# Batch 0's first two x pieces by another queue and another engine, filter copies between bt copies, and w1 - w2 in quarters

## The chip, the cores and the metric

The kernel runs on one core of a Trainium2 chip. The metric is the device time of one execution in microseconds; a profiled execution also gives a span, from the first to the last instruction that its trace holds. The engines are called TensorE (PE in the profile; its weight loads are PEld), VectorE (DVE), ScalarE (ACT), GpSimd (POOL) and SyncE (SP). DMAs are issued by SyncE (queue q1 in the profile) and by GpSimd (queue q0); both share the core's 16 DMA engines.

## What is computed

Eight batches of 3072 tokens with 256 channels are filtered along the sequence in the frequency domain, and the result goes through a max-out layer:

```python
X = np.fft.rfft(x, axis=1)
Y = X * (filt_r + 1j * filt_i)
y = np.fft.irfft(Y, n=3072, axis=1)          # 8 x 3072 x 256
g = np.maximum(y @ w1, y @ w2)               # 256 -> 1024
out = g @ w_out                              # 1024 -> 256
```

Since max(a, b) = b + max(a - b, 0), the kernel needs one wide product: y @ (w1 - w2), a Relu, the product with w_out, and y @ M with M = w2 @ w_out.

## The kernel before

**Tiling.** A sequence of 3072 is split as 96 x 32. The transform is two matmul stages with tables (`C1`, `U`), a product with the filter `F`, and two stages back (`VP` and `VQ`, then `G1`). Batch 1 is transformed while batch 0 goes through the max-out layer, batch 2 while batch 1 does, and so on. The tables, batch 0's whole transform and the weights come first, and nothing runs beside them: this is the prologue, the code from line 143 to line 651. After it the loop at line 693 runs 64 steps of 384 tokens, each with eight `moe_h` (L448, the product with `Wd` = w1 - w2) and the thirty matmuls of `moe_o` (L474 and L476) for the step before. The order of the program is written by hand, and each engine executes its own instructions in that order.

**The prologue in its order.**

- GpSimd issues eight DMAs of batch 0's x (`load_x`, L88), each 96 rows of 1024 numbers, cast from float32 to bfloat16 on the way, with the index tables (iota) between them. Then come 18 DMAs of the filter (`load_f`, L117, L120, L124): ten for the part `WP[0]` (frequency blocks w = 0 to 7), eight for `WP[1]` (w = 8 to 11). Then the first quarter of batch 1's x (L172).
- VectorE builds the angles of `C1` (L176 to L184) and of `U` (L201 to L239). The latter need four small ScalarE results `t2` (L219).
- ScalarE computes `C1` by a sine (L185), those four, and later the two halves of `U` (L243).
- `s1t(c)` for c = 0 to 7 (L495): eight matmuls of an x piece with `C1`, and two evictions (L505 on ScalarE, L503 on VectorE for the last two pieces) into `at2`. `spin` puts filler matmuls between them.
- `t1(n)` for n = 0 to 5 (L507) transposes `at2`; VectorE (even n, L516) and ScalarE (odd n, L514) copy the results to `bt`.
- The filter has to stand on 64 partitions although 32 are loaded: `double_f` copies the other 32, by four VectorE copies for `WP[0]` (L130) and by four SyncE DMAs for `WP[1]` (L132). `fix_f` (L140) sets one row.
- `s2` (L376) makes `px`; the products with `F` (L382, L388, L389) are shared between VectorE, which reads `px` in PSUM, and GpSimd, which reads a copy `xs` that ScalarE makes (L593). GpSimd has v = 0, 2, 3, 4 and half of 5.
- `s3t`, `t2` and `s4` lead to the first tile of y, which the first `moe_h` reads.
- GpSimd, after its last product, issues two quarters of batch 1's x (L633), makes the first half of `Wd` (`prep_wd(0, G)`, L292, 128 x 1024 numbers), issues `Wo` (L288) and the last quarter of batch 1's x, makes the second half of `Wd`, and then the table `CT`.

**What reads these.** `moe_h(0, j)` reads 128 columns of `Wd`: j = 0 to 3 the first half, 4 to 7 the second. The first `moe_o` and `prep_m` (L306) read `Wo`. `f1(1, c)` (L324) reads batch 1's x: c = 0 to 3 the first quarter, 4 to 7 the second, and so on; c = 4 comes in step 3 of the loop, c = 8 in step 6.

```python
    def prep_wd(h, engine):
        js = slice(512 * h, 512 * h + 512)
        engine.tensor_tensor(Wd[:, :, js], w1f[:, :, js], w2f[:, :, js], OP.subtract)
```

Of the kernel before, what the change touches and what calls it, by code (L numbers as in the profile page):

```python
# [10 lines left out]
AF = mybir.ActivationFunctionType  # L11
# [6 lines left out]
NP = 96  # L18
NM = 32
# [7 lines left out]
def kernel(  # L27
# [14 lines left out]
    nc = tc.nc  # L42
    V, S, G, TE = nc.vector, nc.scalar, nc.gpsimd, nc.tensor
# [20 lines left out]
    XF = [const.tile([128, 2, 2, D], FP32, name="XF%d" % k) for k in range(3)]  # L64
# [11 lines left out]
    xb = {}  # L76

    def x_tile(b, c):
        if c % 2 == 0:
            xb[b] = xpool.tile([128, 8, D], BF16, tag="xb", name="xb")  # L80
        return xb[b][:, 4 * (c % 2):4 * (c % 2) + 4]

    def load_x(b, c, n):
        for k in range(c, c + n):
            xb[b, k] = x_tile(b, k)[0:NP]
        src = x[b].rearrange("(p m) d -> p m d", m=NM)
        m0 = 4 * (c % 2)
        G.dma_start(out=xb[b][0:NP, m0:m0 + 4 * n], in_=src[:, 4 * c:4 * c + 4 * n, :])  # L88

    def load_xf(b, c):  # L90
        src = x[b].rearrange("(h p m) d -> p h m d", h=2, m=NM)
        for g in range(2):
            nc.sync.dma_start(out=XF[(8 * b + c) % 3][64 * g:64 * g + 48],
                              in_=src[:, :, 4 * c + 2 * g:4 * c + 2 * g + 2, :])
            if b == 2 and c < 3:

                nc.sync.dma_start(out=XF[(8 * b + c) % 3][64 * g + 48:64 * g + 64],
                                  in_=src[0:16, :, 4 * c + 2 * g:4 * c + 2 * g + 2, :])
# [27 lines left out]
    def double_f(h, g, ri, engine):  # L126
        w0, w1 = WP[h]
        o_, i_ = F[64 * g + 32:64 * g + 64, ri, w0:w1], F[64 * g:64 * g + 32, ri, w0:w1]
        if engine is V:
            V.tensor_copy(o_, i_)  # L130
        else:
            nc.sync.dma_start(out=o_, in_=i_)  # L132
# [3 lines left out]
    def load_fn():  # L136
        nc.sync.dma_start(out=FN[32:33], in_=filt_r[1536:1537, :])

    def fix_f():
        V.tensor_copy(F[32:33, 0, 0, 0], FN[32:33])  # L140
# [9 lines left out]
    cid = init.tile([128, 128], FP32)  # L150

    hv = init.tile([128, 2, 1], FP32)
    load_x(0, 0, 1)
    G.iota(pid, pattern=[[1, 1]], base=0, channel_multiplier=1, allow_small_or_imprecise_dtypes=True)
    G.iota(kc, pattern=[[2, NW], [24, 2], [1, 2]], base=0, channel_multiplier=0,
           allow_small_or_imprecise_dtypes=True)
    load_x(0, 1, 1)
    G.iota(kap, pattern=[[2, NW], [24, 2]], base=0, channel_multiplier=0,
           allow_small_or_imprecise_dtypes=True)
    G.iota(jb, pattern=[[1, 16]], base=0, channel_multiplier=0, allow_small_or_imprecise_dtypes=True)  # L160
    load_x(0, 2, 1)
    G.iota(cid, pattern=[[1, 128]], base=0, channel_multiplier=0, allow_small_or_imprecise_dtypes=True)
    for c in range(3, 8):
        load_x(0, c, 1)
    for q in range(2):
        G.memset(hv[:, q], 1.0)
# [2 lines left out]
    load_f(0)  # L169
    load_f(1)  # L170
    load_fn()
    load_x(1, 0, 2)  # L172

    def table_c():
        p96 = init.tile([128, 1], FP32)
        V.tensor_scalar(p96, pid, 1.0 / 96.0, None, OP.mult)  # L176
        uc = init.tile([NP, 48, 2], FP32)
        rc = init.tile([NP, 48, 2], FP32)
        kf = kc.rearrange("p w g s -> p (w g s)")
        V.tensor_scalar(uc[:, :, 0], kf, p96[0:NP], 0.25, OP.mult, OP.add)  # L180
        V.tensor_scalar(uc[:, :, 1], kf, p96[0:NP], None, OP.mult)
        V.tensor_scalar(uc[:, 0:1, 1], pid[0:NP], 0.5, 0.25, OP.mult, OP.add)
        V.tensor_scalar(rc, uc, RND, RND, OP.add, OP.subtract)
        V.tensor_tensor(uc, uc, rc, OP.subtract)  # L184
        S.activation(C1, uc.rearrange("p k r -> p (k r)"), AF.Sin, bias=zero[0:NP], scale=TWO_PI)  # L185

    def table_ct():
        G.memset(CT, 0.0)
        for g in range(2):
            G.tensor_copy(CT[64 * g:64 * g + 48, :, 0:48].rearrange("p s (u r) -> p s u r", r=2),  # L190
                          C1[0:48].rearrange("p (u s r) -> p s u r", s=2, r=2))
# [49 lines left out]
    def sines_u(h):  # L241
        uv = ua.rearrange("p u c s j -> p u (c s j)")
        S.activation(U[:, NW * h:NW * h + NW], uv[:, NW * h:NW * h + NW], AF.Sin, bias=zero, scale=TWO_PI)  # L243

    def table_g():
        pg = ps.tile([96, NP], FP32, tag="ps", name="pg")
        TE.matmul(pg, C1, I128[0:NP, 0:NP], start=True, stop=True)
        S.activation(G1, pg, AF.Copy)
# [30 lines left out]
    def load_w(h):  # L279
        js = slice(512 * h, 512 * h + 512)  # L280
        nc.sync.dma_start(out=w1f[:, :, js], in_=moe_w1.rearrange("(c p) j -> p c j", p=128)[:, :, js])
        nc.sync.dma_start(out=w2f[:, :, js], in_=moe_w2.rearrange("(c p) j -> p c j", p=128)[:, :, js])
# [4 lines left out]
    def load_wo():  # L287
        G.dma_start(out=Wo, in_=moe_w_out.rearrange("(c p) j -> p c j", p=128))  # L288

    def prep_wd(h, engine):  # L290
        js = slice(512 * h, 512 * h + 512)
        engine.tensor_tensor(Wd[:, :, js], w1f[:, :, js], w2f[:, :, js], OP.subtract)  # L292

    def prep_t(jp):
# [212 lines left out]
    def t1(n, engine):  # L507
        pb = ps.tile([128, 4, D], BF16, tag="ps", name="pb")
        for i in range(4):
            for dc in range(2):  # L510
                TE.transpose(pb[:, i, 128 * dc:128 * dc + 128],
                             at2[:, dc, 4 * n + i].rearrange("p q m -> p (q m)"), I128)
        if engine is S:
            S.activation(bt[0][:, 4 * n:4 * n + 4], pb, AF.Copy)  # L514
        else:
            V.tensor_copy(bt[0][:, 4 * n:4 * n + 4], pb)  # L516

    def s3t(v, pq):
        pool, tag = (ps, "ps") if v % 2 else (pso, "po")
        pz = [pool.tile([128, 2, 2, 2, 2, NM], FP32, tag=tag, name="pt%d" % g) for g in range(2)]  # L520
        for _ in range(2 if v == 1 else 1):
            TE.matmul(pz[0].rearrange("p i s r c m -> p (i s r c m)"), W1[:, 0:128], W1, start=True, stop=True)
        for i in range(2):
            for s in range(2):
                for dc in range(2):
                    for q, tab in enumerate((VP, VQ)):
                        for g in range(2):
                            TE.matmul(pz[g][:, i, s, :, dc], pq[s][64 * g:64 * g + 64, q, i, 128 * dc:128 * dc + 128],  # L528
                                      tab[64 * g:64 * g + 64, 2 * v + i, s].rearrange("p (r m) -> p r m", r=2),
                                      start=(q == 0), stop=(q == 1))  # L530
        zv = zT.rearrange("p c m (w g) q -> p w g (c m) q", g=2)
        for g in range(2):
            o_ = zv[:, 2 * v:2 * v + 2, g]
            i_ = pz[g].rearrange("p i s r c m -> p i (c m) (s r)")
            if v >= 4 and g == 1:
                V.tensor_copy(o_, i_)
            else:
                S.activation(o_, i_, AF.Copy)
# [17 lines left out]
    def spin(n):  # L556
        for _ in range(n):
            pd = ps.tile([128, 512], FP32, tag="ps", name="pd")
            TE.matmul(pd, W1[:, 0:128], W1, start=True, stop=True)  # L559
# [8 lines left out]
            double_f(1, g, ri, nc.sync)  # L568
    for h in range(2):
        load_w(h)  # L570
    spin(12)
    for c in range(8):
        s1t(c)
        if c == 0:
            table_g()
        if c == 4:
            sines_u(0)
        if c < 7:
            spin(2)
    bt[0] = bpool.tile([128, NU, D], BF16, tag="bt", name="bt")  # L580
    for n in range(6):
        t1(n, S if n % 2 else V)
    put_v(0, 0, table_v(0, 0))
    for g in range(2):
        for ri in range(2):
            double_f(0, g, ri, V)
            if g == 0 and ri == 0:
                fix_f()
    xs = {}

    def stage_x(v):
# [6 lines left out]
    def products(v):  # L598
        pool = pq0 if v > 2 else pqpool
        pq = [product(V, v, 0, pxs[v][0], pool)]  # L600
        if v == 5:
            pq.append(shared_product(v, 1, pxs[v][1], xs[v], pool))
        else:
            pq.append(product(G, v, 1, xs[v], pool) if v in POOLED else product(V, v, 1, pxs[v][1], pool))
        return pq
# [11 lines left out]
    put_v(1, 1, table_v(1, 1))  # L617
    for v in (1, 0, 2):
        pqs[v] = products(v)
    s3t(1, pqs[1])  # L620
    pxs[4] = s2(0, 4)
    stage_x(4)
# [7 lines left out]
        pqs[v] = products(v)  # L630
    for v in (4, 5):
        s3t(v, pqs[v])
    for c in (2, 4):  # L633
        load_x(1, c, 2)
    prep_wd(0, G)
    load_wo()
    load_x(1, 6, 2)
    prep_wd(1, G)
    table_ct()
    setup.close()  # L640
    apool = ctx.enter_context(tc.tile_pool(name="apool", bufs=3))
# [51 lines left out]
    for tt in range(8 * B + 1):  # L693
        b, i = divmod(tt, 8)
        k = 0
        for j in range(8):
# [5 lines left out]
            if tt > 0:  # L702
                n = 3 if j in (3, 7) else 4
# [36 lines left out]
```

## Time and profile before

| | us |
|---|---|
| median of 3 runs | 504.27 (502.98 to 505.7) |
| the profiled execution | 503.8 |
| its span | 502.0 |
| TensorE busy in the span | 488.4 (97%) |
| TensorE busy, first 50 us | 40.25 |
| TensorE busy, 50 to 60 us | 10.00 of 10 |
| VectorE, ScalarE, GpSimd busy in the span | 331.9, 308.3, 257.5 |

A line of the timeline gives start, duration, engine, source line, operation, what it writes and reads, and in brackets the idle time of that engine before it and what ended it. The chain of waits is followed back from the last instruction; each piece has a start, a duration and what ran or was waited for.

### The profile page before, as it was taken

To read this page: it belongs to the slowest core of one execution; us is meant where nothing else is said; L and a number is where in the kernel's file an instruction comes from. 1 tells how busy PE (TensorE), PEld (TensorE's weight loads), DVE (VectorE), ACT (ScalarE), POOL (GpSimd) and SP (SyncE) were. 2 spreads that over 40 slices of the span, in tenths; PEclk is the share of its full clock that TensorE was granted. 3 is DMA by queue.
4 is the path that set the end of the run, shared out by engine and by line. 5 is a ranking of instruction groups with operands and counts; after the bars stand their busy time and mean duration, and the time that the engine had idled before them with its cause. 6 is when DMAs were issued, how large, how long until landed. Compare 5 with 4: busy or idle time off the path is not lost.

```text
span 502.0 us, 13079 instructions
## 1 busy us (share of the span) xinstructions
PE 488.4 (97%) x5299; PEld 362.1 (72%) x5303; DVE 331.9 (66%) x518; ACT 308.3 (61%) x629; POOL 257.5 (51%) x338
## 2 busy tenths in 40 slices
PE   8688999999999999999999999999999999999997
PEld 3455777777777777777777777777777777777775
DVE  7876688457865777457765687557765687555553
ACT  6776478647774676557764586647774465544442
POOL 7893569547463864645654855537632221222220
PEclk9989999999999999999999999999999999999999
DMA  7999789995799667986779558896769235411112
GB/s 125 150 252 217 230 229 290 306 274 171 212 268 260 175 204 234 250 229 189 198 244 275 187 177 245 235 239 197 197 181 255 78 111 153 168 65 64 64 64 84
DMA packets 77966, 97.20 MB, mean 194 GB/s; under 512 B 8017, under 2 KB 54354, under 8 KB 77842
## 3 DMA queue, kind: packets, MB, share of 16 engines
q1 hardware_dynamic: 64642, 66.73, 49.6%
q0 software_dynamic: 13264, 29.64, 20.3%
q8 instruction: 41, 0.67, 0.6%
q14 instruction: 19, 0.16, 0.1%
HBM read 53.87 MB, written 47.19 MB: 201 GB/s over the span
## 4 chain that ended last, share of the span: by engine, by line
PE 90%; DMA 5%; POOL 2%; issue 1%; ACT 1%; DVE 0%; SPq 0%; POOLq 0%; DVEq 0%
PE po L476 34%; PE ph L448 33%; PE po L474 8%; PE pz L399 5%; PE py L428 4%; PE pa L349 2%; DMA F<-in_filt_r_dram 2%; PE px L376 2%; DMA Wo<-in_moe_w_out_dram 2%; POOL xb L88 1%; DMA F<-F 1%; PE pr L549 1%; POOL pq L382 0%; PE pt L528 0%; PE pm__1132 L306 0%
## 5 line engine op out<-in xcount | busy, mean ns | idle before, releaser
L476 PE MATMUL po<-Wo,gt 128*128 128x256 bf16 x1536 | 261.0, 273 | 0.2 <-DMA Wo<-in_moe_w_out_dram 0.2
L452 ACT ACTIVATE gt<-ph 128x384 bf16<-128x384 f32 x321 | 157.0, 496 | 147.9 <-PE ph L448 147.3
L461 POOL DMA_DIRECT2D out_dram<-ot x186 | 102.6, 555 | 187.1 <-DVE ot L488 184.4
L476 PEld LDWEIGHTS <-gt 128*128 128x128 bf16 x1536 | 146.6, 98 | 66.1 <-issue 10.3
L450 DVE TENSOR_SCALAR gt<-ph 128x384 bf16<-128x384 f32 x191 | 104.9, 552 | 63.1 <-PE ph L448 59.9
L382 DVE TENSOR_TENSOR pq<-px,F 128x1024 bf16<-128x1024 f32 x91 | 107.0, 1219 | 24.2 <-PE px L376 22.6
L448 PEld LDWEIGHTS <-Wd 128*128 128x128 bf16 x1024 | 96.5, 98 | 12.9 <-POOL Wd L292 1.4
L103 POOL TENSOR_TENSOR xb<-XF 128x512 bf16<-128x512 f32 x48 | 61.2, 1276 | 41.3 <-DMA XF<-in_x_dram 21.2
L488 DVE COPY ot<-po 128x512 f32<-128x512 f32 x95 | 65.1, 685 | 25.3 <-PE po L476 25.0
L104 POOL TENSOR_TENSOR xb<-XF 128x512 bf16<-128x512 f32 x48 | 61.0, 1271 | 0.0
L403 ACT ACTIVATE zt<-pz 128x512 bf16<-128x512 f32 x84 | 45.6, 595 | 11.5 <-PE pz L399 8.4
L353 ACT ACTIVATE at<-pa 128x512 bf16<-128x512 f32 x96 | 51.8, 610 | 1.2 <-PE pa L349 0.8
L428 PE MATMUL py<-G,zr 96*128 96x96 bf16 x512 | 32.7, 206 | 0.2
L428 PEld LDWEIGHTS <-zr 96*128 96x128 bf16 x512 | 29.0, 97 | 2.5 <-DVE zr L552 0.4
L399 PE MATMUL pz<-pq,VP 64*64 64x256 bf16 x336 | 21.9, 281 | 0.0
L376 PE MATMUL px<-bt,U 64*64 64x256 bf16 x384 | 19.8, 278 | 1.2 <-ACT VQ L273 0.7
L399 PE MATMUL pz<-pq,VQ 64*64 64x256 bf16 x336 | 20.9, 269 | 0.0
L349 PE MATMUL pa<-xb,CT 64*64 64x512 bf16 x192 | 19.5, 383 | 0.0
L399 PEld LDWEIGHTS <-VP 64*64 64x64 bf16 x336 | 9.7, 105 | 13.3 <-issue 13.3
L376 PEld LDWEIGHTS <-U 64*64 64x64 bf16 x384 | 10.4, 109 | 3.9 <-issue 3.3
L559 PE MATMUL pd<-W 128*128 128x512 bf16 x30 | 10.5, 462 | 1.7 <-DVE zero L145 1.5
L552 DVE COPY zr<-pr 96x1024 bf16<-96x1024 bf16 (+1 forms) x8 | 5.2, 649 | 8.0 <-PE pr L549 8.0
(429 smaller groups left out, 609.7 us busy)
## 6 DMA issues: line engine op xcount, KB each, us to landing
out_dram<-ot POOLq DMA_DIRECT2D x186, 128.0 KB, 3.3
XF<-in_x_dram SPq DMA_DIRECT2D x96, 192.0 KB, 4.6
ad<-at SPq DMA_DIRECT2D x56, 192.0 KB, 3.3
bt<-ad SPq DMA_DIRECT2D x14, 768.0 KB, 9.1
zd<-zt SPq DMA_DIRECT2D x42, 256.0 KB, 2.7
zr<-zd SPq DMA_DIRECT2D x56, 192.0 KB, 4.8
WS<-in_moe_w_dram SPq DMA_DIRECT2D x4, 512.0 KB, 5.1
xb<-in_x_dram POOLq DMA_DIRECT2D x8, 192.0 KB, 5.8
```

Of the source, the lines that this page charges most:

```text
L103: G.tensor_tensor(t_[:, 0], f[:, 0], f[:, 1], OP.add)
L104: G.tensor_tensor(t_[:, 1], f[:, 0], f[:, 1], OP.subtract)
L353: S.activation(at[:, m0:m0 + 2], pa[g], AF.Copy)
L382: E.tensor_tensor(pq, px.rearrange("p (o i) d -> p o i d", o=1).to_broadcast([128, 2, 2, D]), F[:, :, 2 * v:2 * v + 2, s], OP.mult)
L399: TE.matmul(pz[g][64 * s:64 * s + 64, i], tab[64 * g:64 * g + 64, 2 * v + i, s], pq[s][64 * g:64 * g + 64, q, i], start=(q == 0), stop=(q ...
L428: TE.matmul(py[:, m], zr[b][:, 4 * i + m, 128 * dc:128 * dc + 128], G1, start=True, stop=True)
L448: TE.matmul(ph, Wd[:, dc, 128 * j:128 * j + 128], y_[:, dc], start=(dc == 0), stop=(dc == 1))
L450: V.tensor_scalar(gt[tt][:, j], ph, 0.0, None, OP.max)
L452: S.activation(gt[tt][:, j], ph, AF.Relu)
L461: E.dma_start(out=dst, in_=ot[tt // 2][:, 3 * (tt % 2) + c])
L476: TE.matmul(p_, g_[:, n - 2, blk], Wo[:, n - 2], start=(e == 0), stop=(e == 9))
L488: V.tensor_copy(ot[tt // 2][:, e - 1:e + 1], po[0])
```

## The change

Batch 0's pieces 0 and 1 are no longer loaded by GpSimd. SyncE loads them as float32, ahead of everything else in its queue, into two of the three buffers `XF` that later batches use, and ScalarE casts them. The cast of piece 0 stands before the sine of `C1`, that of piece 1 right behind it. Pieces 2 to 7 stay with GpSimd, and the iotas stand between them as before. In the built program ScalarE's order begins with a table load, the cast of piece 0, a second table load, the sine of `C1`, the cast of piece 1, the four `t2`; before, it began with one table load and the sine.

`s1t` runs in the order 0, 2, 1, 3 to 7; the first filler has nine matmuls in place of twelve; `table_g` comes after piece 2; the first half of `U` comes after all of `s1t` instead of after piece 4.

VectorE's order in the `t1` stage becomes: copy of `F` (group 0, real), `fix_f`, bt 0, copy of `F`, bt 2, copy of `F`, bt 4, copy of `F`. Before, it was bt 0, 2, 4, then the copies.

GpSimd: the first quarter of batch 1's x is issued after the product of v = 0 instead of before all products. After the last product, the order is quarter 0 of `Wd`, x quarter 2, quarter 1 of `Wd`, x quarter 3, `Wo`, quarter 2 of `Wd`, x quarter 4, quarter 3 of `Wd`.

```diff
+    def load_x0(c):
+        xb[0, c] = x_tile(0, c)[0:NP]
+        nc.sync.dma_start(out=XF[c][0:NP].rearrange("p a b d -> p (a b) d"),
+                          in_=x[0].rearrange("(p m) d -> p m d", m=NM)[:, 4 * c:4 * c + 4, :])
+
+    def cast_x0(c):
+        S.activation(xb[0, c], XF[c][0:NP].rearrange("p a b d -> p (a b) d"), AF.Copy)
...
-    load_x(0, 0, 1)
+    for c in range(2):
+        load_x0(c)
+    load_x(0, 2, 1)
...
-    load_x(1, 0, 2)
...
+        cast_x0(0)
         S.activation(C1, uc.rearrange("p k r -> p (k r)"), AF.Sin, bias=zero[0:NP], scale=TWO_PI)
+        cast_x0(1)
...
-        js = slice(512 * h, 512 * h + 512)
+        js = slice(256 * h, 256 * h + 256)
...
-    spin(12)
-    for c in range(8):
+    spin(9)
+    for c in (0, 2, 1, 3, 4, 5, 6, 7):
         s1t(c)
-        if c == 0:
+        if c == 2:
             table_g()
-        if c == 4:
-            sines_u(0)
         if c < 7:
             spin(2)
+    sines_u(0)
     bt[0] = bpool.tile([128, NU, D], BF16, tag="bt", name="bt")
     for n in range(6):
+        if n % 2 == 0:
+            double_f(0, n // 4, n // 2 % 2, V)
+        if n == 0:
+            fix_f()
         t1(n, S if n % 2 else V)
     put_v(0, 0, table_v(0, 0))
...
+    double_f(0, 1, 1, V)
...
     for v in (1, 0, 2):
         pqs[v] = products(v)
+        if v == 0:
+            load_x(1, 0, 2)
...
-    for c in (2, 4):
-        load_x(1, c, 2)
     prep_wd(0, G)
+    load_x(1, 2, 2)
+    prep_wd(1, G)
+    load_x(1, 4, 2)
     load_wo()
+    prep_wd(2, G)
     load_x(1, 6, 2)
-    prep_wd(1, G)
+    prep_wd(3, G)
     table_ct()
```

More of the change, by code (lines that the diff above doesn't have):

```diff
@@ L156 @@
            allow_small_or_imprecise_dtypes=True)
-    load_x(0, 1, 1)
+    load_x(0, 3, 1)
     G.iota(kap, pattern=[[2, NW], [24, 2]], base=0, channel_multiplier=0,
@@ L160 @@
     G.iota(jb, pattern=[[1, 16]], base=0, channel_multiplier=0, allow_small_or_imprecise_dtypes=True)
-    load_x(0, 2, 1)
+    load_x(0, 4, 1)
     G.iota(cid, pattern=[[1, 128]], base=0, channel_multiplier=0, allow_small_or_imprecise_dtypes=True)
-    for c in range(3, 8):
+    for c in range(5, 8):
         load_x(0, c, 1)
@@ L570 @@
         load_w(h)
-    spin(12)
-    for c in range(8):
+    spin(9)
+    for c in (0, 2, 1, 3, 4, 5, 6, 7):
         s1t(c)
-        if c == 0:
+        if c == 2:
             table_g()
-        if c == 4:
-            sines_u(0)
         if c < 7:
             spin(2)
+    sines_u(0)
     bt[0] = bpool.tile([128, NU, D], BF16, tag="bt", name="bt")
     for n in range(6):
+        if n % 2 == 0:
+            double_f(0, n // 4, n // 2 % 2, V)
+        if n == 0:
+            fix_f()
         t1(n, S if n % 2 else V)
     put_v(0, 0, table_v(0, 0))
[L584 to L588, printed above, removed]
+    double_f(0, 1, 1, V)
     xs = {}
```

## The prediction

> **What bounds the kernel now.** First the page's shares, then the windows, then the chain. TensorE is busy 97% of the span, and 10.00 of 10 us from 50 to 60 us, but 40.25 of the first 50. The change edits only those first 50 us, so I predict when TensorE's dense stretch begins; what follows has the same instructions and moves with it. The chain of waits says what stands ahead of it:
>
> ```profile
> 30.64 2.10 POOL pq L382
> 32.73 1.15 POOL pq L389
> 33.88 1.00 POOL xb L88 x2
> ...
> 37.19 9.41 DMA Wo<-in_moe_w_out_dram
> 46.60 0.04 issue
> 46.64 0.60 PE po L476 x4
> ```
>
> GpSimd's products end at 33.88, two x quarters and half of Wd follow, then Wo: issued at 37.19, landed at 46.60, and TensorE's first po waits for it. That wait is short (0.18 us of idle), so Wo and TensorE's own chain (product, y, eight ph) end nearly together. GpSimd's timeline shows what precedes the products:
>
> ```profile
> 17.69 0.53 POOL L120 DMA_DIRECT2D F<-in_filt_i_dram  x1
> 18.22 1.25 POOL L117 DMA_DIRECT2D F<-in_filt_r_dram  x1
> ...
> 22.28 1.17 POOL L120 DMA_DIRECT2D F<-in_filt_i_dram  x1
> 23.43 0.52 POOL L88 DMA_DIRECT2D xb<-in_x_dram  x1
> 24.02 2.13 POOL L382 TENSOR_TENSOR pq<-xs,F 128x1024 bf16<-128x1024 f32 x1
> ```
>
> The first product comes right behind the x issue at 23.43. The filter issues take 1.2 to 1.5 us instead of 0.5 from 18.2 on, when VectorE's filter copies (18.15 to 23.32, 1.22 each) run. ScalarE's start:
>
> ```profile
> 0.75 1.28 ACT L185 ACT_TABLE_LOAD   x1 [0.75 <-PEq L724]
> 3.94 0.38 ACT L185 ACTIVATE C<-uc,zero 96x96 bf16<-96x96 f32 x1 [1.91 <-DVE uc L184]
> ```
>
> One table load, hidden in the wait for VectorE; C1 stands at 4.32. The first s1t starts at 6.13 behind the fillers, the last eviction ends at 14.99, each piece waiting for its DMA (landings 4.9, 6.8, 8.1, 9.7, 10.8, 11.7, 12.7, 13.8).
>
> **Step 1, ScalarE's head.** SyncE issues piece 0 at 0.75, where FN stood. No row has this transfer: the GpSimd piece of the same source bytes took 3.6 us from issue to landing, the shortest of half its size on SyncE 2.9, the third GpSimd piece 4.6. I take 3.6, its nearest row: landing at 4.35 (3.65 to 5.35). The cast: 1.02, by ScalarE's 128x1024 row (L300). Then the second table load, 1.28 by its row, and the sine, 0.38: C1 at 7.03 instead of 4.32. Behind it stand the cast of piece 1 (1.02, to 8.05) and the four t2 (1.36, to 9.41). Queued behind these: all evictions of s1t, 14 at 0.42 and G at 0.23, to 15.5; before, their end was 14.75. So ScalarE replaces the DMA as the pace of s1t, and the earlier transfers win nothing there. VectorE waits for t2: its angle work, 8.25 to 13.30 before from the end of L228 on, now begins at 9.7 and ends at 14.8, still ahead of its two evictions. at2 is complete at 15.5 instead of 14.99: **+0.5**.
>
> [...] The trace shows 1.28 for the load and cannot show a tail: the sine had to wait for VectorE 1.9 us longer anyway. [...]
>
> **Step 2, VectorE's copies.** From 15.5: four filter copies (4 x 1.22), fix_f 0.28, three bt copies (3 x 0.69), 7.2, with gaps 7.4, to 22.9. Before, the last copy ended at 23.32, as VectorE waited 0.66 for the first transpose at 15.64; now the first filter copy covers that (its DMAs landed by 15.7 before, and will be earlier). **-0.4**. What waits for bt now: px for v = 0 and xs. ScalarE has the sine of U (0.94, moved behind s1t) to 16.5, three bt copies (2.85) to 19.3, VP (1.26) to 20.6, xs to about 21.6, ahead of 22.9: hidden by 1.3 us; beyond that it would cost one for one.
>
> **Step 3, GpSimd's products.** Two issues of 0.53 fewer stand ahead, and fewer filter issues meet a copy, so its issues end well before 22.9. Products started 0.50 after the last copy on VectorE: start 23.4 instead of 24.02 (-0.6). The x issue now lies between the products (+0.53). The wait of 0.31 before v = 4, for the doubling DMAs, goes, as they follow the filter issues (-0.3). The last product ends at 33.5 instead of 33.88: **-0.4**. That quarter of x is wanted at 34.3; issued at 25.6 with the old 5.3 to landing it is there at 30.9: free.
>
> **Step 4, TensorE up to Wo.** The first ph came 3.6 after the last product: 37.1. A quarter of Wd is half of 2.36, 1.18, by its own row, or 1.28 by the 128x512 row of L103; I take 1.18. Quarter 0 stands at 34.7, the others at 36.5, 39.1, 40.9, each before its ph. The wait of 0.67 for the second half at 41.07 goes. TensorE is then at the first po 0.4 + 0.67 = 1.07 earlier, near 45.5.
>
> **Step 5, what is late next: Wo.** GpSimd's queue is served in order: from 33.84 on its four transfers were issued as x, x, Wo, x and landed at 39.1, 41.0, 46.6 and 49.0, and the queue took 88% or more of the engines' time from 35 to 45. Its start therefore sets Wo, not Wo's own issue (37.0 instead of 37.19). The first x quarter leaves 1.18 later relative to the last product, as a Wd quarter stands ahead of it: 34.7 instead of 33.84. Wo lands at 46.6 + 0.85 = 47.45. f1 number 4 wants that x quarter at 39.65 and gets it at 39.95, a wait that Wo covers. **+0.85**, bounded by -0.7 and +1.0 from step 1's landing.
>
> **The sum**: -0.4 (product chain) + 1.18 (Wd quarter ahead of x), rounded to +0.85, on the profiled execution's 503.8: 504.65. That execution is 0.47 below the median of the runs shown, 504.27, so the forecast for the median is **505.1**; its own range, by step 1's bounds, 504.4 to 506.1. Fillers, the order 0, 2, 1 and FN's later place cost nothing: ScalarE's 0.86 per piece covers the first two, and FN is read only at 16.7.
>
> **Rivals**, on the median.
>
> - *Wo is not late* (0.18). If the x quarters run faster with the weight loads finished earlier, TensorE's own chain decides: -1.07, 503.2. For it: Wo's wait was only 0.18 us. Against it: SyncE's queue had been nearly empty since 35, and Wo still took to 46.6.
> [...]
> - *A slow TensorE in s1t* (0.13), the slower side. Fillers now end near 5.3 and the first piece waits to 7.1. Weight loads took 0.15 until 5.6 and 0.10 after, so TensorE starts at a lower speed (the clock column misses that), and it can fall back:
>
> ```profile
> 22.00:23.00 1.00, 0.00 (x0) 0.00 (x0) 1.00 (x2) 1.00 (x2) 1.00 (x2) 0.87 0.94 190
> 23.00:24.00 1.00, 0.62 (x32) 0.51 (x32) 0.50 (x2) 0.37 (x2) 0.95 (x2) 0.50 0.75 172
> ...
> 29.00:30.00 1.00, 0.89 (x28) 0.62 (x23) 0.56 (x1) 0.47 (x2) 1.00 (x1) 0.72 0.97 324
> 30.00:31.00 1.00, 0.81 (x25) 0.41 (x26) 0.40 (x1) 1.00 (x3) 0.69 (x2) 1.00 0.99 379
> ```
>
>   The columns are window, length, busy time of TensorE, its weight loads, VectorE, ScalarE and GpSimd, granted clock, DMA share, GB/s. After a gap of 1.5 us it ran at 0.50 for some 6.6 us. A piece then takes 2 x 0.51 and two fillers at 0.43, 1.88, over ScalarE's 0.86. For 6.6 us from 7.1 on: 3.5 pieces, then 4.5 at 0.86, an end near 17.8, +2.3: 507.4. It decides from the point where the slow stretch outlasts ScalarE's backlog, about 11. Against it: work from 1.47 to 5.3 is nearly what sufficed before.
> - *The load is early and unused*: this is in the forecast, for C1 stands behind the first cast.
>
> **Chances.** Forecast 0.52, rivals 0.18, 0.15, 0.13, others 0.02. A measurement of this kernel tells about 0.5%, 2.5 us, from no change. Faster by more: 0.02, there is no case for it. Slower by more: the slow TensorE and a third of the table case, 0.18. Within: 0.80. Range 503.0 to 507.2: it takes in the first rival and the table tail and leaves out most of the slow clock.
>
> **What would show it.** [...] Weight loads of 0.15 in s1t would show the slow clock. The forecast is wrong if the first po starts before 46.6, or if a later stage does not move with it.

## The result and the profile after

The changed kernel takes 506.49 us (median of 11 runs, 505.72 to 507.88); the kernel before, run beside it, 504.26 (502.98 to 506.08). The ratio is 1.0043, 95% interval 1.0028 to 1.0059: slower by 0.28% to 0.59%, 2.2 us by the medians. The profiled execution took 506.41, its span 504.6 (before: 503.8 and 502.0). From 50 to 60 us TensorE is busy 10.00 of 10 us in both, and the first po is 2.44 later in a span 2.6 longer: nearly the whole difference arises in the prologue, as forecast. Some 0.2 us follow behind it: at 65.63 TensorE waits 0.22 for the `bt` of batch 1, which comes by DMA (`bt<-ad`), and it has no such wait before.

The chain of waits of the changed kernel, the part that answers to the chain shown of before by its longest pieces (start, duration, what ran or was waited for):

```profile
20.17 0.72 ACT VP L285 x2
20.93 0.45 PE px L388 x7
21.41 0.60 ACT xs L604
...
31.11 0.50 ACT xs L604
31.68 1.97 POOL pq L394
33.76 1.17 POOL pq L401
...
36.09 0.56 POOL xb L88
36.66 1.28 POOL Wd L304
37.95 0.46 POOL xb L88
38.41 10.63 DMA Wo<-in_moe_w_out_dram
49.08 0.60 PE po L488 x4
```

Its end is as the prediction had it: product, `Wd` quarter, x quarter, `Wo`, first po. All of it is later: `Wo` lands at 49.04 instead of 46.60 (47.4 forecast), and a wait of 0.59 stands before the first po (1.95 by steps 4 and 5). What is new stands above it. Before, the chain came to GpSimd's last products through the doubling DMAs of the filter and a product of VectorE; now it comes through ScalarE and TensorE, which take turns from the eviction of VP on, and `F` is not in it.

GpSimd's timeline shows the same from its side:

```profile
23.71 2.12 POOL L394 TENSOR_TENSOR pq<-xs,F 128x1024 bf16<-128x1024 f32 x1 [4.00 <-ACT VQ L285]
...
31.68 2.13 POOL L394 TENSOR_TENSOR pq<-xs,F 128x1024 bf16<-128x1024 f32 x1 [1.09 <-ACT xs L604]
```

The idle time in the first line is 4.00, for the filter issues ahead of it are over at 19.7 instead of 23.45, and the first product starts 0.31 earlier than before. But the product of v = 4 waits 1.09 for its copy `xs` and ends later. Before, it had waited 0.31; VectorE's product of v = 4 waited 1.03 there for the doubling DMAs and started at 30.60, within 0.03 of GpSimd's at 30.63. ScalarE's head:

```profile
4.70 1.06 ACT L97 ACTIVATE xb<-XF 96x1024 bf16<-96x1024 f32 x1 [2.67 <-DMA XF<-in_x_dram]
5.77 1.28 ACT L196 ACT_TABLE_LOAD   x1
7.07 0.37 ACT L196 ACTIVATE C<-uc,zero 96x96 bf16<-96x96 f32 x1
```

Piece 0 lands 3.92 after its issue at 0.75, and C1 ends at 7.44. Where the time comes in, from both traces:

| event, us | before | after | shift |
|---|---|---|---|
| at2 complete | 14.99 | 15.91 | +0.92 |
| xs of v = 0 ends | 20.43 | 22.01 | +1.58 |
| xs of v = 2 ends | 22.50 | 25.09 | +2.59 |
| xs of v = 4 ends | 29.01 | 31.60 | +2.59 |
| GpSimd's product of v = 4 starts | 30.63 | 31.68 | +1.05 |
| GpSimd's last product ends | 33.89 | 34.93 | +1.04 |
| first x quarter after it is issued | 33.83 | 36.09 | +2.26 |
| Wo lands | 46.60 | 49.04 | +2.44 |
| span | 502.0 | 504.6 | +2.6 |

ScalarE's chain loses 2.59. Before, xs of v = 4 lay ready 1.62 us ahead of GpSimd, now 0.08, so 1.54 of the loss is absorbed and 1.05 passes on. The quarter of `Wd` ahead of the x quarter adds 1.2.

The place where the chain loses time is between the first two `xs`. ScalarE's timeline before:

```profile
19.79 0.64 ACT L593 ACTIVATE xs<-px 128x512 f32<-128x512 f32 x1
20.64 0.40 ACT L272 ACTIVATE VQ<-pv,zero,hv 128x64 bf16<-128x64 f32 x1 [0.22 <-PE pv L263]
...
21.90 0.60 ACT L593 ACTIVATE xs<-px 128x512 f32<-128x512 f32 x1
```

and after:

```profile
21.41 0.60 ACT L604 ACTIVATE xs<-px 128x512 f32<-128x512 f32 x1 [0.53 <-PE px L388]
22.85 0.40 ACT L284 ACTIVATE VQ<-pv,zero,hv 128x64 bf16<-128x64 f32 x1 [0.85 <-PE pv L275]
...
24.49 0.60 ACT L604 ACTIVATE xs<-px 128x512 f32<-128x512 f32 x1 [0.53 <-PE px L388]
```

The durations are nearly the same; the idle times in brackets were 0.22 in all and are now 1.91, for before each of these steps ScalarE waits for TensorE. That is 1.69 more, and the chain lost 1.67 behind at2 (2.59 less 0.92). What TensorE waits for at the same place, before (the `px` of v = 2):

```profile
21.43 0.41 PE L376 MATMUL px<-bt,U 64*64 64x256 bf16 x7 [0.68 <-ACT VQ L273]
```

and after (the `px` of v = 0, the second table's `pv`, the `px` of v = 2):

```profile
20.55 0.79 PE L388 MATMUL px<-bt,U 64*64 64x256 bf16 x8 [0.21 <-ACT VP L285]
22.05 0.19 PE L273 MATMUL pv<-I,U 64*32 64x64 bf16 x1 [0.72 <-ACT xs L604]
...
23.63 0.79 PE L388 MATMUL px<-bt,U 64*64 64x256 bf16 x8 [1.03 <-ACT VQ L285]
```

The waits in the built programs tell why. `px`, the tables' `pv` and the transposes' `pb` share one PSUM pool (a set of buffers for TensorE's results), and a buffer is handed on when its last reader is done. With VectorE's bt copies spread out by filter copies, other buffers come free first. Before, px of v = 0 took buffers that wait for bt copies, pv of the second table those that wait for the evictions of VP, and px of v = 2 one that waits for xs of v = 0 and one that waits for the first half of VQ. After, px of v = 0 waits for both halves of VP, one half of the second table's pv for xs of v = 0, and px of v = 2 for both halves of VQ. Each TensorE group now waits for the ScalarE step just ahead of it, and ScalarE's next step waits for that group.

### The profile page after: what moved, and what is told of

The parts are those of the page before. It is cut to its first block, busy times and chain, and to the rows that moved or that the text cites. A ratio compares the mean times of both kernels' runs of the same rounds, so it can differ in the third digit from the quotient of the medians.

```text
span 504.6 us, 13082 instructions
## 1 busy us (share of the span) xinstructions
PE 488.9 (97%) x5300; PEld 362.6 (72%) x5300; DVE 332.4 (66%) x518; ACT 311.4 (62%) x632; POOL 255.5 (51%) x338
## 4 chain that ended last, share of the span: by engine, by line
PE 88%; DMA 5%; ACT 3%; DVE 2%; POOL 1%; issue 1%; SPq 0%; ACTq 0%; DVEq 0%
PE po L488 33%; PE ph L460 32%; PE po L486 8%; PE pz L411 5%; PE py L440 4%; PE pa L361 2%; PE px L388 2%; DMA Wo<-in_moe_w_out_dram 2%; DMA bt<-ad 1%; DMA XF<-in_x_dram 1%; DMA ad<-at 0%; PE pr L561 0%; ACT bt L526 0%; DVE ua L240 0%; ACT xb L97 0%
## 5 line engine op out<-in xcount | busy, mean ns | idle before, releaser
L388 PEld LDWEIGHTS <-U 64*64 64x64 bf16 x384 | 10.4, 108 | 5.6 <-issue 4.5
L571 PE MATMUL pd<-W 128*128 128x512 bf16 x28 | 10.5, 479 | 1.5 <-DVE zero L154 1.5
L394 POOL TENSOR_TENSOR pq<-xs,F 128x1024 bf16<-128x1024 f32 x4 | 8.5, 2132 | 5.1 <-ACT VQ L285 4.0
```

What stands on the lines that cost most here:

```text
L394: E.tensor_tensor(pq, px.rearrange("p (o i) d -> p o i d", o=1).to_broadcast([128, 2, 2, D]), F[:, :, 2 * v:2 * v + 2, s], OP.mult)
```

## The experiments

Four theories. **A**: the chain of ScalarE and TensorE is late, by at2 and by these PSUM buffers, and the new order behind the last product then delays `Wo` by about one `Wd` quarter. **B**: that order alone. **C**: the first 16 us (cast, table load, at2) alone. **D**: TensorE at half its clock (granted 0.50 instead of 1.00). In the table, "over before" is the difference of medians against the kernel before on the same chip; the times in the prologue are those of the profiled execution, which can lie away from the median.

| kernel | median | over before | ratio, 95% | at2 | xs of v = 4 ends | last product ends | first po |
|---|---|---|---|---|---|---|---|
| after | 506.49 | +2.23 | 1.0028 to 1.0059 | 15.91 | 31.60 | 34.93 | 49.08 |
| tail_alone | 505.28 | +0.83 | 0.9990 to 1.0029 | 15.13 | 29.39 | 33.30 | 47.83 |
| x_ahead | 506.16 | +1.71 | 1.0017 to 1.0042 | 16.21 | 31.75 | 35.08 | 48.56 |
| late_cast | 504.93 | +0.48 | 0.9994 to 1.0021 | 15.67 | 31.44 | 34.77 | 48.62 |
| copies_last | 506.74 | +2.29 | 1.0019 to 1.0059 | 17.90 | 31.92 | 36.50 | 49.63 |
| tables_other_psum | 505.96 | +1.52 | 1.0010 to 1.0057 | 15.89 | 29.55 | 33.67 | 46.95 |
| pso_xfirst | 505.51 | +1.07 | 0.9994 to 1.0028 | 16.74 | 30.51 | 34.52 | 47.80 |
| more_fill | 505.71 | +1.27 | 1.0007 to 1.0040 | 15.80 | 31.57 | 34.89 | 48.36 |
| loads_back | 507.61 | +3.17 | 1.0040 to 1.0082 | 16.08 | 31.89 | 36.88 | 50.55 |
| fill_tables | 504.27 | +0.39 | 0.9996 to 1.0029 | 15.68 | 29.55 | 33.42 | 47.30 |
| fill_tables_x | 504.31 | +0.43 | 0.9997 to 1.0017 | 16.09 | 29.86 | 33.83 | 46.68 |
| early_queue | 504.15 | +0.27 | 0.9994 to 1.0012 | 16.29 | 30.22 | 33.84 | 47.65 |
| early_queue_late | 504.91 | +1.03 | 0.9998 to 1.0044 | 14.93 | 28.56 | 34.31 | 47.33 |

**tail_alone**: the kernel before with nothing but the new order behind the last product.

```diff
-    for c in (2, 4):
-        load_x(1, c, 2)
     prep_wd(0, G)
+    load_x(1, 2, 2)
+    prep_wd(1, G)
+    load_x(1, 4, 2)
     load_wo()
+    prep_wd(2, G)
     load_x(1, 6, 2)
-    prep_wd(1, G)
+    prep_wd(3, G)
```

> The kernel before, with only GpSimd's new order after the last product (a quarter of Wd ahead of each x quarter). Theory A (two causes: a chain of ScalarE and TensorE that ends later, and this order, which delays Wo): the first x quarter leaves some 1.2 to 1.3 us later (35.1 instead of 33.84), Wo lands near 47.9 and the first po starts there instead of at 46.64: +1.2, about 505.5. Theory B (this order is the whole cause): +2.2, 506.5. Theory C (all of it is made in the first 16 us, by the casts and the table load): 0, 504.3.

Its first x quarter leaves at 35.27 instead of 33.83, `Wo` lands at 47.79, and TensorE waits for it. Of those 1.44, 0.77 is a wait of GpSimd for the loads of w1 and w2 at 34.06; the last product ended 0.59 earlier than before.

```profile
47.83 0.60 PE L476 MATMUL po<-Wo,gt 128*128 128x256 bf16 x4 [0.95 <-DMA Wo<-in_moe_w_out_dram]
```

The order costs 1.2 us at the first po and +0.83 in the median, about the size that the prediction gave the whole change. It leaves 1.4 of the 2.2 unexplained, and B's 2.2 lies outside its interval (up to 1.46): B falls. C, which expects nothing here, is at odds with the trace, where the first po is 1.19 late with the head as before; the interval of the median still takes in no change.

**x_ahead**: the changed kernel with x quarters 2 and 3 again ahead of the first quarter of `Wd`.

```diff
+    for c in (2, 4):
+        load_x(1, c, 2)
     prep_wd(0, G)
-    load_x(1, 2, 2)
     prep_wd(1, G)
-    load_x(1, 4, 2)
     load_wo()
-    prep_wd(2, G)
     load_x(1, 6, 2)
+    prep_wd(2, G)
     prep_wd(3, G)
```

> The changed kernel, with the two x quarters issued ahead of the first quarter of Wd again, as before. Theory A: the first x quarter leaves at about 35 instead of 36.1, Wo lands near 47.9, but TensorE's own chain is only ready near 48.5: the first po at 48.5 instead of 49.08, -0.6, about 505.9, and the first ph stays at 39.7. Theory B: back to before, -2.2, 504.3. Theory C: no change from the changed kernel.

`Wo` now takes 7.8 us instead of 10.6 and is there first; the first po starts at 48.56 without a wait for it, and the time falls by 0.3 to 0.5 only. Taking the new order back helps little, because TensorE's own chain is as late as `Wo`. The two limits stand side by side, and each hides the gain of removing the other.

**late_cast**: the changed kernel with the cast of piece 0 behind the sine, and so with one table load.

```diff
-        cast_x0(0)
         S.activation(C1, uc.rearrange("p k r -> p (k r)"), AF.Sin, bias=zero[0:NP], scale=TWO_PI)
+        cast_x0(0)
         cast_x0(1)
```

> The changed kernel, with the cast of piece 0 behind the sine of C1, so that ScalarE has one table load. C1 ends at 4.3 instead of 7.44, the second cast at 6.8, t2 at 8.1 instead of 9.5, at2 is complete near 14.7 instead of 15.93. Theory A: everything behind moves by that, first po near 47.9, -1.2, about 505.3. Theory B: no change. Theory C: -1.2 as well, and then all that is left over before is the order of GpSimd's tail. Theory D (a slow TensorE is the cause: half clock from 7.9 to 11.3 and from 25.0 to 31.6): the first slow stretch goes, as the first piece follows the fillers at once, and the second moves; the gain is then more than the 1.2 us by which at2 is earlier.

C1 ends at 4.31 and t2 at 8.57 (after: 7.44 and 9.54), and the median falls by 1.6. The profiled execution is the slowest of its 12 runs (506.53) and shows at2 at 15.67, only 0.24 earlier, since TensorE fell to half its clock from 8.5 to 12.25; behind the prologue it also waits 0.46 at 74.69 for GpSimd. So the head matters in the median, by more than the 0.92 that the traces show at at2; this trace can't show where the rest sits.

**copies_last**: the changed kernel with the four filter copies behind all bt copies again.

```diff
     for n in range(6):
-        if n % 2 == 0:
-            double_f(0, n // 4, n // 2 % 2, V)
-        if n == 0:
-            fix_f()
         t1(n, S if n % 2 else V)
     put_v(0, 0, table_v(0, 0))
-    double_f(0, 1, 1, V)
+    for g in range(2):
+        for ri in range(2):
+            double_f(0, g, ri, V)
+            if g == 0 and ri == 0:
+                fix_f()
```

> The changed kernel, with VectorE's filter copies behind all its bt copies, as before. In the built program the products' inputs then wait for the bt copies alone, and no longer for the evictions of VP, xs and VQ, whose PSUM buffers they got. Theory A, with that as the cause of ScalarE's late chain: xs for v = 4 ends near 30.0 instead of 31.6, the first ph starts near 38.7 instead of 39.7; but the filter copies end near 24.3 instead of 23.5, so that GpSimd's last product ends near 35.0 as it does now, and Wo stays at 49: total within 0.4 of the changed kernel. If the chain is late only for its late start (Theory C): xs for v = 4 stays at 31.6. If the new order of copies was a gain by itself: slower by 0.8.

Its runs fall into two groups, 504.8 to 505.0 and 506.6 to 508.3. The profiled one is of the second: TensorE ran at half its clock from 8.5 to 15.5, at2 is complete at 17.90. From at2 to xs of v = 4 it takes 14.0, as before (14.0), while the changed kernel takes 15.7: the buffers are as before again, and the 1.7 is gone. But the last filter copy ends at 26.24 and the products at 36.50. Counted from at2, the first product comes 0.72 later without the interleaving (8.52 and 7.80), the last ends 0.42 earlier (18.60 and 19.02): the interleaving brings the products' start forward, and the order of the buffers takes more than that from their end. That the interleaving serves the products once the buffers are others shows only in the next run, where the last one ends 17.78 after at2.

**tables_other_psum**: the changed kernel with the first halves of the tables in the other PSUM pool.

```diff
-        pool, tag = (pso, "po") if h else (ps, "ps")
+        pool, tag = pso, "po"
```

> The changed kernel, where the first two tables V get their PSUM from the pool that is still unused at that time, in place of the buffers that they share with px. In the built program px for v = 0 then waits for bt copies alone, the second table for VP, px for v = 2 for xs of v = 0, as before the change. Theory A (PSUM buffers that came free late tie ScalarE and TensorE into one chain): xs for v = 4 ends near 29.5 instead of 31.6, GpSimd has no wait of 1.1 before v = 4, its last product ends near 33.9 instead of 34.9, Wo lands near 48: -1.1, about 505.4. Theory C (the late start in the first 16 us is all): xs for v = 4 and the total stay.

ScalarE's timeline:

```profile
20.70 0.64 ACT L604 ACTIVATE xs<-px 128x512 f32<-128x512 f32 x1
21.59 0.41 ACT L284 ACTIVATE VQ<-pv,zero,hv 128x64 bf16<-128x64 f32 x1 [0.26 <-PE pv L275]
...
22.58 0.61 ACT L604 ACTIVATE xs<-px 128x512 f32<-128x512 f32 x1
```

The idle times of 0.53, 0.85 and 0.53 are gone but for one of 0.26. With at2 at 15.89, as in the changed kernel, xs of v = 4 ends 2.05 earlier, GpSimd waits for nothing, and the last product ends at 33.67. In the trace the mechanism of A is shown: this execution took 503.99. It is also the fastest of its 12 runs, and the median shows the gain less well: 505.96, with an interval that overlaps that of the changed kernel. The runs lie between 503.99 and 508.41, and the four above 507 have TensorE's mean granted clock at 0.983 to 0.987, the other eight at 0.988 to 0.996, so the spread goes with TensorE's clock.

**pso_xfirst**: the last kernel with the x quarters ahead as well (both diffs above).

> The same, with the x quarters ahead of the first quarter of Wd again. Theory A: the first x quarter leaves near 33.9 and Wo lands near 46.8, with TensorE ready at about the same time: -2.2 against the changed kernel, about 504.3, the time before, though at2 is still complete at 15.9. Theory C: at least the 0.9 us by which at2 is late remains, 505.2 or more.

At 505.51 it is 1.2 above the 504.3 expected. The profiled execution took 505.71, 1.72 more than that of the last kernel, and two places account for nearly all of it, neither touched by the edits. at2 is complete at 16.74, 0.85 later, because TensorE is slow from its start to about 13: a piece takes 0.84 at 10.45 and 0.50 at 14.09, two fillers 1.05 at 11.09 and 0.60 at 14.43. The column of the granted clock shows 1.00 there. The other 0.80 lies behind the prologue: at 64.93 TensorE waits that long for batch 1's `bt`, as it does for 0.22 in the changed kernel.

**more_fill**: the changed kernel with 18 fillers at the start instead of 9.

```diff
-    spin(9)
+    spin(18)
```

> The changed kernel with 18 filler matmuls at the start in place of 9, to keep TensorE busy until C1 is there. Theory D (the half clock in the s1t stage costs time): the slow stretch from 7.75 to 11.5 goes and the total falls by 1 us or more. Theory A: ScalarE's backlog hides that stretch; it goes, at2 is complete at most 0.4 earlier, and the total moves by 0.4 at most; only the spread of the runs may shrink.

Windows with the columns that the prediction's have; the third number from the end is the granted clock. After:

```profile
8.00:9.00 1.00, 1.00 (x8) 0.50 (x6) 0.29 (x1) 1.00 (x4) 0.74 (x3) 0.50 1.09 195
```

With 18 fillers:

```profile
8.00:9.00 1.00, 0.89 (x12) 0.49 (x11) 0.43 (x2) 1.00 (x4) 0.98 (x3) 1.00 1.12 205
```

The changed kernel's slow stretch there (7.75 to 11.25, after a gap of 2.46) is gone. In this pair of executions at2 gains only 0.11, since ScalarE is busy from 7 to 12 either way; but the runs draw together (505.15 to 506.19), and the median falls by 0.8, or by 0.96 when each is taken against the kernel before beside it. The two intervals overlap (1.0007 to 1.0040 and 1.0028 to 1.0059). By the medians D is a part of the loss and not the whole; that it comes from slow stretches which outlast ScalarE's backlog in some executions fits copies_last and is not shown here.

**loads_back**: the changed kernel with all eight pieces loaded by GpSimd again and no casts.

```diff
-    for c in range(2):
-        load_x0(c)
-    load_x(0, 2, 1)
+    load_x(0, 0, 1)
...
-    load_x(0, 3, 1)
+    load_x(0, 1, 1)
...
-    load_x(0, 4, 1)
+    load_x(0, 2, 1)
...
-    for c in range(5, 8):
+    for c in range(3, 8):
...
-        cast_x0(0)
         S.activation(C1, uc.rearrange("p k r -> p (k r)"), AF.Sin, bias=zero[0:NP], scale=TWO_PI)
-        cast_x0(1)
```

> The changed kernel with all eight pieces of batch 0's x by GpSimd again, no casts, one table load, everything else as changed. Theories A and C: C1 ends at 4.3, at2 is complete near 15.0 instead of 15.9, and all that follows is 0.9 earlier: 505.6. If the pieces by SyncE are a gain in themselves, as they let the filter come earlier: slower than the changed kernel, since the filter copies then wait.

Of the two outcomes expected, the gain didn't come and the loss, by filter copies that wait, did: it became the slowest kernel of all, +3.17. C1 (4.30) and t2 (7.44) are as before and at2 is only 1.09 later, so C, by which all the loss lies there, falls. VectorE and GpSimd:

```profile
17.05 1.22 DVE L139 COPY F<-F 32x4096 bf16<-32x4096 bf16 x1 [0.97 <-DMA F<-in_filt_r_dram]
```

```profile
24.59 0.54 POOL L129 DMA_DIRECT2D F<-in_filt_i_dram  x1
25.20 2.13 POOL L390 TENSOR_TENSOR pq<-xs,F 128x1024 bf16<-128x1024 f32 x1
```

With two issues more ahead of them, the filter's transfers arrive after the point where VectorE now wants them: the first copy waits 0.97. GpSimd's issues last to 25.1 instead of 19.7, and the products start at 25.2. The order 0, 2, 1 is kept here, and TensorE waits 2.15 for piece 2, which makes at2 late. Further on GpSimd's product of v = 4 waits 1.53 for the doubling DMAs. The SyncE loads are what lets filter copies stand between bt copies; the parts of the change need each other.

**fill_tables**: 18 fillers and the tables in the other pool, the new order behind the products kept.

> The changed kernel with 18 filler matmuls at the start instead of 9, and with both halves of the spectrum's tables taken from the other PSUM pool, so that px of v = 0 no longer stands behind the eviction of VP. Theory A (buffers and ScalarE's order make the product chain late): the first slow TensorE stretch is gone as with 18 fillers alone, xs of v = 4 ends near 29.5 instead of 31.6, v = 4 doesn't wait for it, the last product ends near 33.8, first po near 47: 504.3 to 504.6, 1.1 to 1.4 below the 505.7 of the 18 fillers alone. A theory that the first 16 us alone set the time (C), or the slow TensorE alone (D): no difference to the 505.7.

504.27, as A had it (504.3 to 504.6), +0.39 over the kernel before beside it; all but one of its runs lie between 503.85 and 504.56. xs of v = 4 ends at 29.55 and v = 4 doesn't wait. Two edits that leave casts, loads, interleaving and `Wd` quarters as they are take back 1.8 of the 2.2. The two ratio intervals just touch (up to 1.0029 here, from 1.0028 after), so the size of that gain is less sure than its sign. From more_fill, which differs by the buffers alone, the time over before falls from 1.27 to 0.39, with intervals that overlap.

**fill_tables_x**: the same with the x quarters ahead.

> As the kernel before this one, with two x quarters ahead of the Wd quarters again. A: Wo lands about 1 us earlier, first po is no longer behind it, TensorE is ready at about 46.7: 504.0 to 504.3, at most 0.4 less than without. If GpSimd's tail were the main loss (B): 503.3 or less.

The first po is at 46.68 without a wait, but the median is the same (504.31). B's 503.3 is out of its interval.

**early_queue**: fill_tables with two x quarters and `Wo` issued in GpSimd's idle time before the products.

```diff
     sines_u(0)
+    load_x(1, 0, 2)
+    load_x(1, 2, 2)
+    load_wo()
...
-        if v == 0:
-            load_x(1, 0, 2)
...
     prep_wd(0, G)
-    load_x(1, 2, 2)
-    prep_wd(1, G)
     load_x(1, 4, 2)
-    load_wo()
-    prep_wd(2, G)
+    prep_wd(1, G)
     load_x(1, 6, 2)
+    prep_wd(2, G)
     prep_wd(3, G)
```

> 18 fillers, tables in the other pool, and the two x quarters and Wo issued in GpSimd's idle time before its products instead of behind them. A: Wo has landed long before 45, no x issue lies between the products, the last product ends near 33.2 and the first po near 46, set by TensorE alone: 503.4. Rival: the x and Wo transfers collide with the filter's doubling DMAs and the loads of w1 and w2 on the DMA engines, so that v = 4 or the Wd quarters wait: 504.3 or more.

The rival came true, and its bound (504.3 or more) was nearly right. `Wo` lands near 40 (issue at 22.41, 17.2 us), but the loads of w1 and w2 take 10.4 us instead of 4.8 in fill_tables, and GpSimd waits for them:

```profile
35.65 1.26 POOL L304 TENSOR_TENSOR Wd<-WS 128x512 bf16<-128x512 f32 x1 [1.81 <-DMA WS<-in_moe_w_dram]
...
39.95 2.68 POOL L304 TENSOR_TENSOR Wd<-WS 128x512 bf16<-128x512 f32 x2 [0.75 <-DMA WS<-in_moe_w_dram]
```

The early issues aren't free on GpSimd either: beside VectorE's filter copies the two x quarters take 1.97 and `Wo` 1.85 (1.06 and 0.93 behind the products in the kernel before), and the first product starts at 24.32 instead of 23.35. One late transfer is exchanged for another. At 504.15 it equals the kernel before within 0.12%.

**early_queue_late**: early_queue with the cast of piece 0 behind the sine, 11 fillers at the start and six behind piece 2.

> As the kernel before this one, with the cast of piece 0 behind the sine (one table load), 11 fillers at the start and six behind piece 2. If ScalarE's head still sets the chain (A): at2 complete near 14.9 instead of 15.8 and first po 0.9 earlier: 502.6. Rival: the head no longer sets it, or TensorE falls back to half its clock in s1t: as the kernel before this one, or slower.

at2 comes 1.36 earlier (14.93) and xs of v = 4 by 1.66, but the last product ends 0.47 later. The chain of waits has no ScalarE in it any more:

```profile
24.32 6.59 DMA F<-F
...
31.07 2.14 POOL pq L394
```

The last doubling DMA of the filter lands at 30.91, and v = 4 waits 1.25 for it. 504.91: the head no longer sets the end of the products; the filter's transfers do. The first po comes 0.32 earlier than in early_queue all the same (47.33), and the span is 0.7 longer: TensorE runs at half its clock from 34.5 to 38.0 and waits 0.96 at 64.62 for batch 1's `bt`. No kernel here is shown to beat the kernel before.

## Why the prediction was nearly right, and where it failed

The time lies in the range, and the mechanism named for the end, `Wo` late by the `Wd` quarter ahead of the x quarter, is the one seen. The sum was 0.85 and the medians say 2.2. That the time is in the range is partly luck: its upper end was there for the table tail (0.15 in the chances), a stop between the second table load and the sine, and left out most of the slow clock, and the waits that made most of the loss had no price in it. No run shows such a stop: the second load begins 0.01 after the cast, takes 1.28, and the sine begins 0.02 after it; in copies_last, tables_other_psum, pso_xfirst and more_fill it begins 0.01 to 0.02 after it.

- *Step 1*, ScalarE's head: +0.5 forecast, +0.92 measured. The transfer of piece 0 took 3.92, not 3.6, and the cast 1.06; t2 ended at 9.54 (9.41) and the evictions at 15.53 (15.5). VectorE is the late one: its angles end at 14.99 instead of 14.8, and its two evictions follow them only at 15.91, which the step had put ahead of ScalarE's end. By its own numbers they would have ended near 15.8, for the two take 1.01 behind 14.8.
- *Step 2*, VectorE's copies: the last ended at 23.53 (22.9 forecast); 0.41 of that comes from at2 and 0.12 from the first copy, which took 1.34. "Hidden by 1.3 us" was true for the first `xs`, at 22.01. Only that one was priced; the later ones hang on it, and the step took TensorE and ScalarE to go on behind it as before.
- *Step 3* is **the step that failed**. The wait of 0.31 before v = 4 was to go and the last product to end 0.4 earlier; it became a wait of 1.09 for xs of v = 4 and an end 1.04 later. tables_other_psum shows the cause: with at2 unchanged and other buffers, xs of v = 4 ends 2.05 earlier and the wait is gone. That term, -0.4 against +1.04, is 1.44 of the 1.76 by which the profiled execution missed the sum (504.65 against 506.41). What the step did not look at is which buffer `px` and `pv` get when VectorE's reads move.
- *Step 4*: no wait for `Wd` before a ph, as forecast. A quarter takes 1.28, the L103 row's value, not 1.18. The first ph came 4.77 after the last product instead of 3.6, because it no longer hangs on it. TensorE's own chain is 2.47 late, as ScalarE's is (px of v = 5 at 31.91 instead of 29.44), and it takes up GpSimd's product of v = 4 at 35.05, 1.24 after that ended and without a wait; before, 0.07 after (32.83 and 32.76). The first ph is 2.22 later (39.70), `Wo` hides that by 0.59, and x_ahead, where `Wo` is in time, shows it. So the 1.07 that this step had TensorE gain never came.
- *Step 5* held: the first x quarter is 2.26 later, and `Wo` lands 2.44 later; in tail_alone 1.44, with the 0.77 of another wait in it, and 1.19. The sum of the step's two terms is 0.78, not 0.85. x_ahead, where the x quarters lead, has no wait for `Wo`.

The rivals. *Wo is not late* is out: a wait of 0.59. *A slow TensorE in s1t* did occur, from 7.75 to 11.25, and ended about where its own condition (about 11) put the end of ScalarE's backlog; at2 gains 0.11 when it is gone (more_fill). In some executions of the variants it lasted longer, as copies_last shows with at2 at 17.90 and pso_xfirst with 16.74. A slow piece with its fillers took 1.5 there (10.45 to 11.94), not 1.88. Of what the steps forecast of the profile, C1 (7.0 forecast, 7.44) and the first product (23.4, 23.71) held, the last product (33.5, 34.93) did not.

Open: how much of the median the head takes in the changed kernel itself (late_cast takes back 1.6, more than its trace shows at at2), and what the other executions of pso_xfirst lost, since the two places found are those of one.

## What to carry to other kernels

When an edit moves the reads of PSUM buffers on one engine, look up which buffers the next tiles get and whom they then wait for; a chain with idle time behind it can turn into two engines taking turns, with no instruction added (here ScalarE's waits for TensorE between two `xs` went from 0.22 to 1.91). Check a slack not at the first consumer but at the last one of the same chain, here xs of v = 4 with 1.6 us to spare. And where two limits lie within a microsecond of each other, undoing the part that made one of them late shows only the distance to the other.

## What the runs showed of the hardware

- TensorE's half-clock stretches (granted clock 0.50) last 3.5 to 3.75, 7.0 to 7.25 or 10.25 to 10.5 us in these traces, in windows of a quarter of a us, and nothing between. Some begin after one gap, of 2.46 in the changed kernel at 7.75; others have no gap above 0.8 shortly ahead of them, as tail_alone's at 21.25, which follows gaps of 0.51 and 0.68. So no single length of gap is the limit here. What sets the lengths of the stretches, and how far the times of the variants differ by them, is not shown.
- The column of the granted clock doesn't show all of it: in pso_xfirst it is 1.00 up to 13 us, while a piece that later takes 0.50 takes 0.84.
- A transfer in flight early was not free: in early_queue `Wo`, issued at 22.41, took 17.2 us instead of 9.8, and the SyncE loads beside it 10.4 instead of 4.8.
